# A list-scheduled attention and FFN kernel: low parts and sums of the FFN's second product shared out anew between VectorE and GpSimd, its first product's last two parts set later, and longer ways between engines in the planner

## The chip, the cores and the metric

One NeuronCore of one Trainium2 chip runs the whole program. The metric is the device time of one execution in microseconds, the median of three runs; the profile is of one further execution. TensorE is PE in the rows (its weight loads are PEld), VectorE is DVE, ScalarE is ACT, GpSimd is POOL, and SyncE, which issues most DMAs, is SP.

## The reference

Causal attention in blocks of 64 over 64 batch-and-head pairs, then a two-layer FFN with a leaky rectifier whose slope `alpha` is given for each hidden unit, all in float32:

```python
# q, k, v: (8, 8, 576, 64); w_in: (512, 2048); w_out: (2048, 512); alpha: (2048,)
scores = 1/sqrt(64) * q @ k.T;  mask: block(i) >= block(j), block of 64
attn = softmax(scores);         x = attn @ v, laid out as (4608 tokens, 512)
h = x @ w_in
g = np.maximum(h, 0.0) + alpha * np.minimum(h, 0.0)
out = g @ w_out
```

## The kernel before

Matrix products run on float32 values split in two: a high part that TensorE takes in its reduced float32 format (`fp32r`) and a low part, the rest. A product is then three: high by high, high by low, low by high. `split` makes the parts: ScalarE casts the high part (line 532), and VectorE or GpSimd subtracts it from the value to get the low part (line 533).

The program has two phases. In the first, attention (lines 979 to 1124) is mixed with the FFN of the first six of the sixteen blocks of 128 hidden units, in chunks of 256 tokens (lines 646 to 679). The other ten blocks, five pairs, come in the second phase in nine rounds of 512 tokens, and both of its products use the Winograd form of Strassen's scheme: seven products of quarter matrices in place of eight.

A round of the second phase has two halves that overlap with those of its neighbours:

- `pair1`, for each of the five pairs of blocks: seven products of six matmuls each (line 722), on three PSUM banks x, y and z. They are numbered 0 to 6 here, as in the code before: x takes 0, 2, 4 and 5, y takes 1, z takes 3 and 6. Between them other engines read the banks: `keep` (ScalarE, line 731) copies x after product 0 (u1), after 2 (u2) and after 4 (u3), and product 2, 4 or 5 may go on adding into x only when that copy is done. VectorE adds z to u3 (line 753), and product 6 may go on in z only after that. `onto` (VectorE, line 735) adds u1 into y and u2 into z. `act` applies the rectifier (ScalarE line 739, VectorE line 740) and leaves four quarters `c` of the hidden values in SBUF.
- `chunk2`, for the 512 tokens: seven products, each a chain of five blocks (one for each pair, index g) of six matmuls (line 780). A block needs the high part `gh` (ScalarE, line 532) and the low part `gl` (line 533) of a quarter or of a sum of quarters. The sums are in `plus` (line 765): three for each pair ahead of product 2 (`second`), one ahead of product 6 (`sums`). Both parts have six buffers. Before the change a low part is made by VectorE for g = 1 and 3 and by GpSimd for g = 0, 2 and 4; in the last round all but g = 0 are VectorE's.

For the next round, `factors` makes sums of quarters of the 512 tokens' input (VectorE, line 549) and splits seven of them: low parts named X, 128 by 512, of which VectorE makes three and GpSimd four (line 533 too).

The order of every engine's instructions is set ahead by `Plan.schedule`, a list scheduler. It keeps a ready queue for each engine by priority (a position on the PE's time axis, such as `turn + k` for product k of `pair1`, `turn + g` for a block of `chunk2` and `t - LEAD` for its split), reckons a cost for every operation (`c_dve`, `c_pool`, `c_act`, and so on), lets a result be seen by another engine `LAT` nanoseconds after its end, and issues what is ready. The engines then run these orders in order, waiting on semaphores. The table `SHIFTS` moves the priorities of single operations of the first phase; the second phase's priorities (from 2.0e6) have no entry in it.

Of the kernel before, what the change touches and what calls it, by code (L numbers as in the profile page):

```python
# [29 lines left out]
CHA = 256  # L30
# [8 lines left out]
BANKS, HB, AB, HT, AM, AT, WB = 7, 2, 2, 3, 2, 3, 4  # L39
LEAD, AHEAD2, XB2, W2N, CN = 6, 12, 10, 11, 6  # L40
# [72 lines left out]
LAT = {"PE": 250, "DVE": 130, "ACT": 140, "POOL": 140}  # L113
# [24 lines left out]
class Plan:  # L138


    def __init__(self):
        self.ops, self.writer, self.readers = [], {}, {}
        self.free, self.tiles, self.quota, self.last = {}, {}, {}, {}
# [11 lines left out]
    def op(self, engine, cost, fn, r=(), w=(), prio=0.0, claim=(), then=None, ends=()):  # L155
# [24 lines left out]
        self.ops.append((engine, cost, fn, deps, bufs, prio, then))  # L180
        return i

    def schedule(self):
# [43 lines left out]
        while events:  # L227
# [13 lines left out]
            for engine, heap in ready.items():  # L241
# [42 lines left out]
                lat = LAT.get(engine, 0)  # L284
# [35 lines left out]
def c_dve(n):  # L320
    return 65 + n / 0.96

# [54 lines left out]
def attn_ffn(ctx, tc, qT, kT, vT, w_in, w_out, alpha, out):  # L377
# [152 lines left out]
    def split(src, hi, lo, n, r, hk, lk, claim, on, prio):  # L530

        op("ACT", c_act(n, True), lambda: nc.scalar.copy(out=hi(), in_=src()), r=r, w=[hk], claim=claim, prio=prio)  # L532
        op(on, c_pool(n) if on == "POOL" else c_dve(n), lambda: (nc.gpsimd if on == "POOL" else nc.vector).tensor_tensor(  # L533
            out=lo(), in0=src(), in1=hi().bitcast(F32), op=ALU.subtract), r=[*r, hk], w=[lk], claim=claim, prio=prio)
# [12 lines left out]
    def add(e, n, to, a, b, f, prio, r=()):  # L547

        op(e, c_pool(n) if e == "POOL" else c_dve(n), lambda: (nc.gpsimd if e == "POOL" else nc.vector).tensor_tensor(  # L549
# [159 lines left out]
    def pair1(f, X, turn):  # L709
# [18 lines left out]
        def keep(bank):  # L728

            u = Buf("g")  # L730
            op("ACT", c_act(CHA), lambda: nc.scalar.copy(out=u(), in_=bank()[:, :CHA]), r=[bank], w=[u], prio=FP)
            return u
# [20 lines left out]
        op("DVE", c_dve(CHA), lambda: nc.vector.tensor_tensor(out=u3(), in0=z()[:, :CHA], in1=u3(), op=ALU.add), r=[z], w=[u3], prio=FP)  # L753
        act(f + 1, u3, u3, cs[3])
        product(x, "22", "t4", 5, False)
        act(f + 1, x, lambda: x()[:, :CHA], cs[2])
        product(z, "s4", "22", 6, False)
# [4 lines left out]
    def chunk2(t0, cs, turn, last):  # L762

        def plus(to, a, b, f, on, prio):
            op(on, c_pool(CHA) if on == "POOL" else c_dve(CHA), lambda: (nc.gpsimd if on == "POOL" else nc.vector).tensor_tensor(  # L765
                out=to(), in0=a(), in1=b(), op=f), r=[a, b], w=[to], prio=prio)

        def product(k, bank, c, at, first):

            for g in range(NG):  # L770
# [4 lines left out]
                split(v, gh, gl, CHA, [v], gh, gl, [], "DVE" if g % 2 or last and g else "POOL", t - LEAD)  # L775
# [37 lines left out]
        def second(g, prio):  # L813

            c11, c12, _, c22, s3 = cs[g]
            plus(s3, c11, c12, ALU.subtract, "DVE", prio)
            plus(c12, c12, c22, ALU.add, "DVE", prio)
            plus(c11, c12, c11, ALU.subtract, "DVE", prio)
# [452 lines left out]
```

## Time and profile before

| | us |
| --- | --- |
| median of three runs | 1119.76 (1118.62 to 1120.52) |
| the profiled execution | 1117.95 |
| span of its instructions | 1115.8 |
| PE busy, PEld busy | 1073.9, 969.9 |
| DVE busy | 814.1 |
| ACT busy | 701.4 |
| POOL busy | 666.2 |
| mean granted TensorE clock | 0.998 |

PE is busy for nearly the whole span, but the ends of its matmuls are modelled, so a stall shows as a gap only where it is longer than what the pipeline hides, and PEld, or the count of matmuls in a stretch, tells more. Attention ends and the second phase begins near 625 us; a round of it is about 53.5 us from then on, so one look at a round stands for the others. A number of nanoseconds after the bar in a group's row is the mean of one instruction; the numbers behind the second bar are the engine's idle time just before the group's instructions, and what ended it.

### The profile page before, as it was taken

Reading aid. Unit: us, or ns where it says so; the run is one execution under the profiler, and the core shown is the slowest. Engines: PE = TensorE matmul, PEld = TensorE weight load, DVE = VectorE, ACT = ScalarE, POOL = GpSimd, SP = SyncE. Lnnn points to the kernel's source line nnn. Section 1 sums busy time; section 2 is a strip of 40 time slices with the busy share of each in tenths; the row PEclk is TensorE's granted clock in tenths of the full one; section 3 lists DMA queues with packets and bytes.
Section 4 is the critical chain, followed back from the end, with each engine's and each line's share of the span. In section 5 each row is a group of like instructions: output and inputs, shape, how many; then the busy total and the mean of one; then the engine's idle time right before and its main releaser. Section 6 shows DMA issues by size and latency. Waiting matters only on the chain.

```text
span 1115.8 us, 24537 instructions
## 1 busy us (share of the span) xinstructions
PE 1073.9 (96%) x8158; PEld 969.9 (87%) x8158; DVE 814.1 (73%) x1779; ACT 701.4 (63%) x1969; POOL 666.2 (60%) x837
## 2 busy tenths in 40 slices
PE   7999999999999999999999989999999999999998
PEld 4668888888888888898888889999989898989998
DVE  8886685676575745757558598879696969787776
ACT  7788877776666766758555564555455555545554
POOL 4767757667676666666489574636272736364522
PEclk9999999999999999999999999999999999999999
DMA  6687886876668795749044436767676868686875
GB/s 193 194 257 214 233 246 169 267 209 194 193 176 248 217 270 157 214 140 271 32 175 152 174 119 199 243 212 243 211 253 202 276 193 280 188 267 196 270 259 162
DMA packets 139486, 233.37 MB, mean 209 GB/s; under 512 B 14816, under 2 KB 51680, under 8 KB 139360
## 3 DMA queue, kind: packets, MB, share of 16 engines
q1 hardware_dynamic: 138928, 231.53, 68.0%
q8 instruction: 65, 1.06, 0.4%
q14 instruction: 61, 0.50, 0.1%
q10 hardware_dynamic: 432, 0.27, 0.1%
HBM read 150.22 MB, written 37.49 MB: 168 GB/s over the span
## 4 chain that ended last, share of the span: by engine, by line
PE 85%; DVE 9%; ACT 2%; issue 2%; DMA 1%; POOL 1%; DVEq 0%; ACTq 0%; POOLq 0%
PE bank L780 17%; PE bank L722 16%; PE bank L646 13%; PE bank L679 13%; PE bank L1120 8%; PE bank L979 6%; PE bank L1019 6%; PE bank L1049 2%; DVE X L533 2%; DVE c L765 2%; PE bank L1076 1%; DVE xt L549 1%; DVE bank L735 1%; PE bank L984 1%; DVE gl L533 1%
## 5 line engine op out<-in xcount | busy, mean ns | idle before, releaser
L722 PE MATMUL bank<-X,w 128*128 128x256 f32 x1890 | 251.7, 284 | 23.0 <-DVE g L753 13.0
L722 PEld LDWEIGHTS bank<-X,w 128*128 128x128 f32 x1890 | 235.2, 189 | 28.8 <-DVE g L753 15.2
L780 PE MATMUL bank<-w,gh 128*128 128x256 f32 x1260 | 228.9, 280 | 0.8 <-ACT gh L532 0.8
L1011 POOL TENSOR_SCALAR p<-p,ri 128x256 f32<-128x256 f32 (+3 forms) x256 | 141.3, 567 | 90.9 <-DVE ri L1009 42.5
L780 PEld LDWEIGHTS bank<-w,gh 128*128 128x128 f32 x1260 | 193.6, 189 | 1.0 <-ACT gh L532 1.0
L780 PE MATMUL bank<-w,gl 128*128 128x256 f32 x630 | 177.6, 282 | 3.5 <-DVE gl L533 3.5
L533 POOL TENSOR_TENSOR gl<-c,gh 128x256 fp32r<-128x256 f32 x112 | 95.2, 855 | 121.4 <-ACT gh L532 120.3
L1003 ACT ACTIVATE p<-bank,nm 128x256 f32<-128x256 f32 (+3 forms) x256 | 133.9, 532 | 28.2 <-DVE nm L1000 13.8
L679 PE MATMUL bank<-wa,gh 128*128 128x512 f32 x432 | 140.1, 405 | 0.0
L646 PE MATMUL bank<-xh,wa 128*128 128x256 f32 x864 | 128.0, 287 | 0.0
L780 PEld LDWEIGHTS bank<-w,gl 128*128 128x128 f32 x630 | 118.9, 189 | 4.7 <-DVE gl L533 4.7
L532 ACT CAST gh<-c 128x256 fp32r<-128x256 f32 x198 | 79.7, 407 | 62.6 <-PE bank L780 60.6
L646 PEld LDWEIGHTS bank<-xh,wa 128*128 128x128 f32 x864 | 113.6, 190 | 2.7 <-issue 0.9
L1019 PE MATMUL bank<-ident,p 128*128 128x128 f32 x640 | 100.2, 277 | 5.0 <-POOL p L1011 2.9
L666 POOL TENSOR_TENSOR gl<-g,gh 128x256 fp32r<-128x256 f32 x108 | 83.2, 773 | 32.4 <-ACT gh L663 26.7
L1000 DVE TENSOR_REDUCE nm<-bank 128x1 f32<-128x384 f32 (+3 forms) x144 | 80.4, 587 | 22.5 <-PE bank L979 18.8
L979 PE MATMUL bank<-K,Q 128*128 128x512 f32 (+1 forms) x448 | 94.5, 331 | 1.1 <-ACT pl L1063 0.9
L1120 PE MATMUL bank<-PTF,vraw 128*64 128x320 f32 (+3 forms) x768 | 94.1, 384 | 0.5 <-ACT PTF L1096 0.5
L1019 PEld LDWEIGHTS bank<-ident,p 128*128 128x128 f32 x640 | 76.0, 142 | 16.8 <-POOL p L1011 6.6
L659 DVE SCALAR_TENSOR_TENSOR g<-g,oal,bank 128x256 f32<-128x256 f32 x108 | 51.4, 476 | 48.3 <-ACT g L657 47.9
L679 PEld LDWEIGHTS bank<-wa,gh 128*128 128x128 f32 x432 | 75.6, 189 | 12.4 <-issue 0.5
L679 PE MATMUL bank<-wa,gl 128*128 128x512 f32 x216 | 85.8, 397 | 0.1
(162 smaller groups left out, 2210.4 us busy)
## 6 DMA issues: line engine op xcount, KB each, us to landing
w<-wd SPq DMA_DIRECT2D x315, 256.0 KB, 4.0
Q<-QH SPq DMA_DIRECT2D x56, 256.0 KB, 3.9
K<-KH SPq DMA_DIRECT2D x112, 128.0 KB, 3.8
vraw<-in_v SPq DMA_DIRECT2D x32, 320.0 KB, 3.7
qraw<-in_q SPq DMA_DIRECT2D x30, 320.0 KB, 4.0
xd<-xT SPq DMA_DIRECT2D x8, 1152.0 KB, 6.5
part<-o SPq DMA_DIRECT2D x36, 256.0 KB, 3.5
xb<-xd SPq DMA_DIRECT2D x9, 1024.0 KB, 7.9
```

The costliest lines, as they stand in the source:

```text
L533: op(on, c_pool(n) if on == "POOL" else c_dve(n), lambda: (nc.gpsimd if on == "POOL" else nc.vector).tensor_tensor(out=lo(), in0=src(), in ...
L646: nc.tensor.matmul(hp()[:, :n], ww()[:, 0, cc * P:(cc + 1) * P], x()[:, cc, :n], start=(i == 0 and cc == 0), stop=(i == 2 and cc == NCC - 1))
L666: op("POOL", c_pool(CHA), lambda: nc.gpsimd.tensor_tensor(out=gl(), in0=g(), in1=gh().bitcast(F32), op=ALU.subtract), r=[g, gh], w=[gl], p ...
L679: nc.tensor.matmul(acc(), a()[:, ts], ww(), start=(first and i == 0), stop=(last and i == 2))
L722: nc.tensor.matmul(bank()[:, :CHA], W()[:, i, 256 * at + P * c:256 * at + P * c + P], B()[:, j, CHA * c:CHA * c + CHA], start=(first and n ...
L780: nc.tensor.matmul(bank()[:, CHA * i:CHA * i + CHA], a()[:, P * i:P * i + P], W()[:, x], start=(first and g + i + n == 0), stop=(g == NG - ...
L979: nc.tensor.matmul(o, Q()[:, i, qs], K()[:, 2 * h + i, :w], start=(i == 0), stop=(i == 1))
L1000: op("DVE", c_dve(w), lambda h=h: nc.vector.tensor_reduce(out=nm()[:, h:h + 1], in_=sb[h]()[:, off[h]:off[h] + w], axis=AX.X, op=ALU.max, ...
L1003: op("ACT", 238 + w / 1.2, lambda h=h, t=t: nc.scalar.activation(out=t()[:, :w], in_=sb[h]()[:, off[h]:off[h] + w], func=AF.Exp, bias=nm() ...
L1011: op("POOL", 244 + w / 1.2, lambda h=h: nc.gpsimd.tensor_scalar(out=pts[h]()[:, :w], in0=pts[h]()[:, :w], scalar1=ri()[:, h:h + 1], scalar ...
L1019: nc.tensor.transpose(out=tp()[:, base + c * P:base + (c + 1) * P], in_=pts[h]()[:, c * P:(c + 1) * P], identity=ident)
L1120: nc.tensor.matmul(ob()[rows[h], a - q0:q1 - q0], V()[:, c, h, :], moving, start=(c == 0), stop=(c == cs[-1][0]))
```

## The change

Four things change together.

- Low parts of `chunk2`: VectorE keeps only g = 1 (`LO_DVE`); g = 0, 2, 3 and 4 are GpSimd's. The last round is as before. In eight rounds that is 56 subtractions.
- Sums of `chunk2` (`SUMS`): two of the three sums of `second` go from VectorE to GpSimd, 90 in all, and the sum of product 6 goes from GpSimd to VectorE, 45 in all.
- In `pair1` products 5 and 6 get the priorities `turn + 6` and `turn + 7` in place of `turn + 5` and `turn + 6`.
- The planner's reckoning: `LAT` is longer for every engine, so that first-phase orders change too; a two-input SBUF operation on VectorE costs 65 + 1.3 n in place of 65 + n / 0.96; and the results of `keep`, of the sum of z and u3, and of the low parts of `chunk2` are reckoned with 500 ns more (`SLACK`) before another engine sees them. These numbers set the order alone.

The lines of the changed kernel stand 11 further down in this part of the code: 722 is 733, 753 is 764, 765 is 776, 780 is 791.

```diff
+SSN, SLACK = 1.3, 500
+SUMS, LO_DVE = ("DVE", "POOL", "POOL", "DVE"), (1,)
...
-LAT = {"PE": 250, "DVE": 130, "ACT": 140, "POOL": 140}
+LAT = {"PE": 320, "DVE": 200, "ACT": 220, "POOL": 220}
...
-        self.ops, self.writer, self.readers = [], {}, {}
+        self.ops, self.writer, self.readers, self.slack = [], {}, {}, []
...
-    def op(self, engine, cost, fn, r=(), w=(), prio=0.0, claim=(), then=None, ends=()):
+    def op(self, engine, cost, fn, r=(), w=(), prio=0.0, claim=(), then=None, ends=(), slack=0):
...
+        self.slack.append(slack)
...
-                lat = LAT.get(engine, 0)
+                lat = LAT.get(engine, 0) + self.slack[chosen]
...
+class SS(float):
+    pass
+
+
+def c_ss(n):
+    return SS(65 + n * SSN)
+
+
...
-    def split(src, hi, lo, n, r, hk, lk, claim, on, prio):
+    def split(src, hi, lo, n, r, hk, lk, claim, on, prio, slack=0):
...
-        op(on, c_pool(n) if on == "POOL" else c_dve(n), lambda: (nc.gpsimd if on == "POOL" else nc.vector).tensor_tensor(
-            out=lo(), in0=src(), in1=hi().bitcast(F32), op=ALU.subtract), r=[*r, hk], w=[lk], claim=claim, prio=prio)
+        op(on, c_pool(n) if on == "POOL" else c_ss(n), lambda: (nc.gpsimd if on == "POOL" else nc.vector).tensor_tensor(
+            out=lo(), in0=src(), in1=hi().bitcast(F32), op=ALU.subtract), r=[*r, hk], w=[lk], claim=claim, prio=prio, slack=slack)
...
-        op(e, c_pool(n) if e == "POOL" else c_dve(n), lambda: (nc.gpsimd if e == "POOL" else nc.vector).tensor_tensor(
+        op(e, c_pool(n) if e == "POOL" else c_ss(n), lambda: (nc.gpsimd if e == "POOL" else nc.vector).tensor_tensor(
...
         def keep(bank):
...
-            op("ACT", c_act(CHA), lambda: nc.scalar.copy(out=u(), in_=bank()[:, :CHA]), r=[bank], w=[u], prio=FP)
+            op("ACT", c_act(CHA), lambda: nc.scalar.copy(out=u(), in_=bank()[:, :CHA]), r=[bank], w=[u], prio=FP, slack=SLACK)
...
         product(z, "s1", "t1", 3, True)
         product(x, "s3", "t3", 4, False)
         u3 = keep(x)
-        op("DVE", c_dve(CHA), lambda: nc.vector.tensor_tensor(out=u3(), in0=z()[:, :CHA], in1=u3(), op=ALU.add), r=[z], w=[u3], prio=FP)
+        op("DVE", c_dve(CHA), lambda: nc.vector.tensor_tensor(out=u3(), in0=z()[:, :CHA], in1=u3(), op=ALU.add), r=[z], w=[u3], prio=FP, slack=SLACK)
         act(f + 1, u3, u3, cs[3])
-        product(x, "22", "t4", 5, False)
+        product(x, "22", "t4", 6, False)
         act(f + 1, x, lambda: x()[:, :CHA], cs[2])
-        product(z, "s4", "22", 6, False)
+        product(z, "s4", "22", 7, False)
...
         act(f, z, lambda: z()[:, :CHA], cs[1])
...
         def plus(to, a, b, f, on, prio):
-            op(on, c_pool(CHA) if on == "POOL" else c_dve(CHA), lambda: (nc.gpsimd if on == "POOL" else nc.vector).tensor_tensor(
+            op(on, c_pool(CHA) if on == "POOL" else c_ss(CHA), lambda: (nc.gpsimd if on == "POOL" else nc.vector).tensor_tensor(
...
-                split(v, gh, gl, CHA, [v], gh, gl, [], "DVE" if g % 2 or last and g else "POOL", t - LEAD)
+                split(v, gh, gl, CHA, [v], gh, gl, [], "DVE" if g in LO_DVE or last and g else "POOL", t - LEAD, SLACK)
...
         def second(g, prio):
...
-            plus(s3, c11, c12, ALU.subtract, "DVE", prio)
-            plus(c12, c12, c22, ALU.add, "DVE", prio)
-            plus(c11, c12, c11, ALU.subtract, "DVE", prio)
+            plus(s3, c11, c12, ALU.subtract, SUMS[0], prio)
+            plus(c12, c12, c22, ALU.add, SUMS[1], prio)
+            plus(c11, c12, c11, ALU.subtract, SUMS[2], prio)
...
         product(5, x, lambda g, prio: cs[g][3], 4, False)
...
-        product(6, z, sums(2, 2, 0, ALU.subtract, "POOL"), 3, False)
+        product(6, z, sums(2, 2, 0, ALU.subtract, SUMS[3]), 3, False)
```

What the scheduler makes of it, at three places of a round in the middle of the second phase. First PE, at the last pair of a round (weights `w13_7265`). In both orders the rows of line 722 or 733 are products 4, 5 and 6, told apart by the bank: x for 4 and 5, z for 6. Four rows of line 780 or 791 are one block of `chunk2`. Before, from product 4 to product 6:

```order
L722 MATMUL bank2_184<-X3_6770,w13_7265 128x256 x6
L780 MATMUL bank0_178<-w211_7288,gh2_680 128x256 x2
L780 MATMUL bank0_178<-w211_7288,gl2_698 128x256
L780 MATMUL bank0_178<-w211_7288,gh2_680 128x256 x2
L780 MATMUL bank0_178<-w211_7288,gl2_698 128x256
L780 MATMUL bank0_178<-w212_7290,gh3_824 128x256 x2
L780 MATMUL bank0_178<-w212_7290,gl3_840 128x256
L780 MATMUL bank0_178<-w212_7290,gh3_824 128x256 x2
L780 MATMUL bank0_178<-w212_7290,gl3_840 128x256
L722 MATMUL bank2_184<-X6_7252,w13_7265 128x256 x6
L722 MATMUL bank7_145<-X5_7247,w13_7265 128x256 x6
```

After, from the second block behind product 4 (which and whose first block stand just ahead of these rows) to product 6:

```order
L791 MATMUL bank1_180<-w29_7267,gh0_537 128x256 x2
L791 MATMUL bank1_180<-w29_7267,gl0_552 128x256
L791 MATMUL bank1_180<-w29_7267,gh0_537 128x256 x2
L791 MATMUL bank1_180<-w29_7267,gl0_552 128x256
L733 MATMUL bank3_186<-X6_7255,w13_7265 128x256 x6
L791 MATMUL bank4_205<-w210_7275,gh1_566 128x256 x2
L791 MATMUL bank4_205<-w210_7275,gl1_574 128x256
L791 MATMUL bank4_205<-w210_7275,gh1_566 128x256 x2
L791 MATMUL bank4_205<-w210_7275,gl1_574 128x256
L733 MATMUL bank2_184<-X0_6729,w13_7265 128x256 x6
```

Between products 4 and 6 stood two blocks and product 5; now there are three blocks and product 5. Ahead of this piece, between products 1 and 4 of the same pair, stood products 2 and 3 and one block, and now there are products 3 and 2 and three blocks.

Second VectorE, at the same pair: from the addition of u1 into y to the sum of z and u3, on which product 6 waits. `X` are low parts of factors, `xt` a sum of factors. Before:

```order
L735 TENSOR_TENSOR bank7_145<-bank7_145,g6_6804 128x256
L765 TENSOR_TENSOR c11_7482<-c5_7359,c11_7482 128x256
L533 TENSOR_TENSOR X2_6753<-xt1_6726,X2_6753 128x512
L740 SCALAR_TENSOR_TENSOR o1_1191<-g4_6761,oal_83,bank7_145 128x256
L549 TENSOR_TENSOR xt1_6726<-xb0_6610,xt1_6726 128x512
L533 TENSOR_TENSOR X4_7241<-xt0_6712,X4_7241 128x512
L753 TENSOR_TENSOR g1_598<-bank1_180,g1_598 128x256
```

After:

```order
L746 TENSOR_TENSOR bank5_211<-bank5_211,g2_715 128x256
L751 SCALAR_TENSOR_TENSOR c10_7439<-g6_6799,oal_83,bank7_145 128x256
L544 TENSOR_TENSOR X2_6777<-xt1_6758,X2_6777 128x512
L751 SCALAR_TENSOR_TENSOR o1_1248<-g0_506,oal_83,bank5_211 128x256
L560 TENSOR_TENSOR xt1_6758<-xb0_6618,xt1_6758 128x512
L544 TENSOR_TENSOR X3_6790<-xt0_6723,X3_6790 128x512
L544 TENSOR_TENSOR gl2_732<-c12_7487,gh2_727 128x256
L776 TENSOR_TENSOR raw0_158<-c16_7576,c10_7439 128x256
L764 TENSOR_TENSOR g4_6756<-bank2_184,g4_6756 128x256
```

One sum of quarters (765) has left its place behind the addition, and a low part, another sum and one more step of the rectifier now stand in the piece.

Third VectorE, a little later, ahead of the addition of u1 into y for the first pair of the next round; the rows of lines 793 and 798 (804 and 809) add a finished product to the output. Before:

```order
L798 TENSOR_TENSOR m1_290<-bank5_211,m1_290 128x512
L765 TENSOR_TENSOR c16_7582<-c17_7546,c16_7582 128x256
L533 TENSOR_TENSOR gl1_631<-raw0_158,gh1_610 128x256
L765 TENSOR_TENSOR raw0_158<-o1_1191,raw0_158 128x256
L765 TENSOR_TENSOR raw0_158<-raw0_158,o0_1179 128x256
L533 TENSOR_TENSOR gl3_840<-c4_7326,gh3_824 128x256
L765 TENSOR_TENSOR o1_1191<-raw0_158,o1_1191 128x256
L793 TENSOR_TENSOR m2_6785<-bank4_207,m2_6785 128x512
L735 TENSOR_TENSOR bank0_178<-bank0_178,g6_6804 128x256
```

After:

```order
L746 TENSOR_TENSOR bank2_184<-bank2_184,g5_6771 128x256
L751 SCALAR_TENSOR_TENSOR raw0_158<-g2_715,oal_83,bank2_184 128x256
L544 TENSOR_TENSOR gl1_574<-raw0_158,gh1_566 128x256
L776 TENSOR_TENSOR raw0_158<-o1_1248,raw0_158 128x256
L804 TENSOR_TENSOR m2_6817<-bank4_205,m2_6817 128x512
L776 TENSOR_TENSOR o1_1248<-o1_1248,c11_7511 128x256
L746 TENSOR_TENSOR bank6_225<-bank6_225,g6_6799 128x256
```

Four sums and two low parts ahead of the addition have become two sums and one low part. On GpSimd, last, the work behind the four X of a round. Before, from the first X on (the sums in it are those of product 6):

```order
L533 TENSOR_TENSOR X1_6733<-xb0_6610,X1_6733 128x512
L533 TENSOR_TENSOR X3_6770<-xb0_6610,X3_6770 128x512
L533 TENSOR_TENSOR X5_7247<-xb0_6610,X5_7247 128x512
L533 TENSOR_TENSOR gl3_840<-c2_7331,gh3_824 128x256
L533 TENSOR_TENSOR X6_7252<-xt1_6726,X6_7252 128x512
L533 TENSOR_TENSOR gl5_1138<-o1_1191,gh5_1120 128x256
L533 TENSOR_TENSOR gl0_506<-c15_7503,gh0_495 128x256
L765 TENSOR_TENSOR raw0_158<-raw0_158,c12_7462 128x256
L533 TENSOR_TENSOR gl2_698<-raw1_176,gh2_680 128x256
L533 TENSOR_TENSOR gl4_951<-c7_7379,gh4_944 128x256
L533 TENSOR_TENSOR gl5_1138<-c11_7482,gh5_1120 128x256
L765 TENSOR_TENSOR c15_7503<-c15_7503,c11_7482 128x256
```

After, the last twelve of the 22 rows that begin with the first X (four X, twelve low parts and six sums):

```order
L544 TENSOR_TENSOR gl2_732<-c13_7479,gh2_727 128x256
L544 TENSOR_TENSOR gl3_852<-raw0_158,gh3_841 128x256
L776 TENSOR_TENSOR c0_7227<-c5_7350,c0_7227 128x256
L776 TENSOR_TENSOR c6_7418<-c1_7320,c6_7418 128x256
L776 TENSOR_TENSOR c9_7430<-c9_7430,o0_1227 128x256
L776 TENSOR_TENSOR c8_7398<-c8_7398,o0_1227 128x256
L544 TENSOR_TENSOR gl5_1120<-c6_7418,gh5_1098 128x256
L776 TENSOR_TENSOR c4_7332<-c9_7430,c4_7332 128x256
L776 TENSOR_TENSOR c3_7298<-c8_7398,c3_7298 128x256
L544 TENSOR_TENSOR gl0_552<-c4_7332,gh0_537 128x256
L544 TENSOR_TENSOR gl1_574<-c3_7298,gh1_566 128x256
L544 TENSOR_TENSOR gl2_732<-raw1_176,gh2_727 128x256
```

In the rows before, sums stand singly between low parts; now six of them, the new ones of `second`, stand close together, each with the low part that needs it some rows behind.

## The prediction

> **What bounds the kernel now.** I read the page first (busy times and the chain that ended last), then the engines by stretches, then who PE waited for, and last the chain through one round.
>
> ```profile
> PE 1073.9 (96%) x8158; PEld 969.9 (87%) x8158; DVE 814.1 (73%) x1779; ACT 701.4 (63%) x1969; POOL 666.2 (60%) x837
> PE 85%; DVE 9%; ACT 2%; issue 2%; DMA 1%; POOL 1%; DVEq 0%; ACTq 0%; POOLq 0%
> ```
>
> PE carries the chain; the change leaves its matmuls as they are, so only stalls can be won. The 9% of DVE in the chain is where PE stood still for it. Two rounds of the second phase (the first and the last of six alike), its first stretches, and one near its end, in the columns stretch, length, PE, PEld, DVE, ACT, POOL, clock, DMA:
>
> ```profile
> 600.00:650.00 50.00, 46.97 (x312) 42.07 (x311) 35.76 (x66) 26.95 (x68) 37.24 (x40) 1.00 0.48 155
> 650.00:700.00 50.00, 44.91 (x365) 43.65 (x364) 43.37 (x78) 27.08 (x74) 27.12 (x27) 1.00 0.54 167
> 703.40:757.00 53.60, 50.93 (x422) 50.28 (x422) 43.75 (x78) 28.93 (x77) 27.17 (x31) 1.00 0.72 227
> 971.20:1024.70 53.50, 50.84 (x422) 50.18 (x422) 43.72 (x78) 28.93 (x77) 27.11 (x31) 1.00 0.73 232
> 1050.00:1100.00 50.00, 50.00 (x421) 49.96 (x420) 37.86 (x77) 26.53 (x71) 16.94 (x21) 1.00 0.82 269
> ```
>
> The stretch at 1050 has 421 matmuls in 50 us with PE full: 118.8 ns each. A round has 420 (35 products and 35 blocks of six), so 49.9 us of work in 53.55 us: 3.65 us are lost in each. From 650 to 700 it is 365 x 118.8 ns = 43.4 us of work, 6.6 us lost. Who PE waited for in six rounds (us, times, longest):
>
> ```profile
> PE bank L722 <- DVE g L753: 7.7, 6, 1.3
> PE bank L722 <- ACT g L731: 5.0, 6, 0.9
> PE bank L780 <- DVE gl L533: 3.5, 6, 0.6
> ACT g L739 <- DVE bank L735: 29.9, 24, 2.6
> ```
>
> Each of the three happens once a round: 1.28, 0.83 and 0.58 us, 2.7 us together. The other 0.95 us of the 3.65 is the pipeline's own start after a stall, some 0.3 us for each, which is shorter than the gaps that are listed. Where the first two come from shows in the chain through 20 us of one round (start, length, what):
>
> ```profile
> 864.42 1.43 PE bank L722 x12
> ...
> 865.94 0.43 DVE bank L735
> 866.37 1.39 DVE c L765
> 867.76 0.60 DVE X L533
> 868.36 0.07 DVE c L740
> ...
> 868.68 1.40 DVE xt L549
> 870.08 1.69 DVE X L533
> 871.76 0.35 DVE g L753
> ...
> 872.15 0.98 PE bank L722 x6
> ...
> 879.85 0.95 DVE c L765
> 880.81 0.60 DVE m L793
> 881.41 0.35 DVE bank L735
> ...
> 882.06 0.38 ACT g L731
> ...
> 882.48 0.97 PE bank L722 x6
> ```
>
> At the last pair of a round products 0 and 1 end at 865.85; from then DVE works without a pause, from the addition into y to the sum for product 6, and product 6 can start only at 872.15. At the next pair the addition into y stands behind DVE's sums; ACT, which has a step of the rectifier ahead of its copy of x, waits for that addition, and PE for the copy. So PE is held by DVE's queue, not by a distance: other pairs have the same distances and no stall.
>
> **The change, part by part: DVE and POOL.** In rounds of the middle VectorE gives up 7 low parts and 10 sums and gets 5 sums. What they cost, from the groups of the six rounds (the number behind the comma is the mean in ns) and from each line by itself (min, median and max in ns):
>
> ```profile
> L533 POOL TENSOR_TENSOR gl<-c,gh 128x256 fp32r<-128x256 f32 x78 | 66.1, 854 | 76.3 <-ACT gh L532 75.4
> L765 POOL TENSOR_TENSOR c<-c,c 128x256 f32<-128x256 f32 x15 | 11.8, 792 | 3.4 <-DVE gl L533 3.4
> L765 DVE TENSOR_TENSOR c<-c,c 128x256 f32<-128x256 f32 x25 | 18.4, 735 | 0.2
> L533 DVE TENSOR_TENSOR gl<-c,gh 128x256 fp32r<-128x256 f32 x50 | 30.8, 615 | 10.1 <-ACT gh L532 9.7
> L740 DVE SCALAR_TENSOR_TENSOR c<-g,oal,bank 128x256 f32<-128x256 f32 x61 | 28.9, 474 | 9.8 <-ACT g L739 9.8
> L532 ACT CAST gh<-c 128x256 fp32r<-128x256 f32 x128 | 51.6, 407 | 40.6 <-PE bank L780 39.6 <-POOL gl L533 0.6
> ...
> L765 DVE TENSOR_TENSOR c<-c,c x25: 406/834/1493, 711.9 to 1018.6; 128x256 f32<-128x256 f32 x25
> L533 POOL TENSOR_TENSOR gl<-c,gh x78: 732/852/1197, 714.3 to 1024.6; 128x256 fp32r<-128x256 f32 x78
> L533 POOL TENSOR_TENSOR X<-xb,X x18: 1292/1459/1754, 705.4 to 976.8; 128x512 fp32r<-128x512 f32 x18
> L533 DVE TENSOR_TENSOR X<-xt,X x12: 679/1221/1773, 706.9 to 977.0; 128x512 fp32r<-128x512 f32 x12
> ```
>
> DVE loses 7 x 0.615 + 5 x 0.735 = 8.0 us of 43.7 a round; POOL gains 7 x 0.854 + 5 x 0.79 = 9.9 us on 27.1, so 37 us in a round that may not be shorter than 49.9. Neither engine is full.
>
> But the same DVE sum takes 0.41 us at the least and 1.49 at the most, and POOL's low part 0.73 to 1.20: operations whose inputs lie in SBUF wait for the other engine's. POOL is busy 27.1 of 53.55 us now (51%) and would be so 37 of some 51 (73%). DVE's sum now costs 0.33 us over its least at 51%; in proportion it would cost 0.47 at 73%, hence 0.88 us, and a low part 0.70. Then 29 operations that take 14 x 0.615 + 15 x 0.735 = 19.6 us become 17 that take 7 x 0.70 + 10 x 0.88 = 13.7 us: 5.9 us less in place of 8.0. I take this value, since both ends of the proportion are rows of this stage; bounds are no dearer at all (8.0) and the longest rows throughout (in rival (a)).
>
> The Trainium skill, "SBUF — State Buffer", section "SBUF: two separate sides", says it harder: VectorE with two SBUF inputs and GpSimd share a port pair by an exclusive lock, and the loser blocks for the whole instruction. The rows with 0.41 beside 1.49 us agree. By that rule alone the time when either holds the pair is what counts: with the least durations, POOL's 21 low parts, 5 sums and 4 X with DVE's 29 and 3 X hold it 24.2 + 13.8 = 38.0 us of 53.55 before, and after, with POOL's 28 low parts, 10 sums and 4 X and DVE's 17 and 3 X, 33.0 + 8.9 = 41.9 us of 49.9 (an estimate). That is an argument against the change, but it still leaves room for a round without stalls.
>
> **PE's order at the three stalls.** The last pair: from the end of product 1 to product 6 there stood products 2, 3, 4 and 5 and three blocks, seven pieces of six matmuls or 0.713 us each: 5.0 us, and with the stall the 6.30 us of the chain (865.85 to 872.15). After, it is the same four products and six blocks, ten pieces or 7.1 us. DVE's work in that time loses a sum (1.39) and gains a step of the rectifier, a low part and a sum, 0.47 + 0.62 + 0.74 = 1.83 us: 6.30 + 0.44 = 6.7 us against 7.1. Hidden, with 0.4 us to spare, if the two X and the `xt` don't get slower; with the longest row for the X that took 0.60 (1.77) it stalls for 0.8 us. I keep 0.5 us of stall and start here on average.
>
> The next pair's copy of x: ahead of the addition into y stand two sums less and one low part less, about 2 us by the means; the stall was 0.83. Gone. The low part that PE waited for 0.58 us was one of VectorE's in the same queue: gone likewise, and what VectorE still makes (g = 1) has a later user. Products 5 and 6, set one later, and the 500 ns put on the two results that PE waited for are what brings blocks in between; they add no instruction.
>
> Covers: VectorE's backlog was POOL's idle time (76.3 us of waiting before low parts in six rounds). What is late next is POOL. Its heaviest stretch is the 22 rows behind the first X: 4 x 1.46 + 12 x 0.854 + 6 x 0.79 = 20.8 us. Their users on PE, with 118.8 ns a matmul, stand 15 us apart in the order, so the stretch must start with 5.8 us in hand. The six buffers let the low part just ahead of it be made some 8.8 us before its use; less the cast (0.41 us by ACT) and itself (0.85) that is 7.5 us. 1.7 us to spare over 22 operations: 0.08 us on each eats it.
>
> I leave 0.8 us of stall a round (0.5 above, 0.3 for POOL and what I can't see): 3.65 - 0.8 = 2.85 us won, in the seven rounds with the stalls (six, and the two stalls that follow at 1024.7): 20.0 us. The first round, 650 to 700, loses 6.6 us, partly because the weights are still being split; of that I take 3. The stretch from 600, where products have no blocks to stand between, I leave.
>
> **The first phase** is ordered anew by the longer `LAT`. PE's waits there, the first two and the last of 14 groups up to 640 us, 12.7 us in all:
>
> ```profile
> PE bank L1019 <- POOL p L1011: 2.9, 2, 2.6
> PE bank L984 <- DVE xT L903: 2.3, 1, 2.3
> ...
> PE bank L984 <- ACT PTF L1096: 0.2, 1, 0.2
> ```
>
> There is hardly anything to win, and much of it is the start, where no order helps. What could be lost is bounded by a first phase as leaky as the second: 3.65 us in 53.55 over 600 us, 41 us. In the order the least PE work between a hidden product (line 646) and the second product that waits for its low part grows from 2.7 to 4.0 us, and that between a score and the transposes that wait for GpSimd's scaling from 3.4 to 4.1 (estimates, matmuls counted and weighed by their spacing here). So I stay near the row: 0, with -3 to +5.
>
> Sum: 1117.95 (span 1115.8 and 2.15 around it) - 20.0 - 3 = 1095. The median of the runs is 1.8 above that execution: 1096.8, so 1097.
>
> **Rivals.** (a) The port eats it. POOL at 73% makes DVE's X and `xt` take their longest: at the last pair 6.7 + 1.2 (the short X) + 0.2 (low part, sum) = 8.1 us against 7.1, a stall of 1.0, nearly as before, and one of the others stays in part. Against it: 5.9 us less work on DVE. Won is about 1.3 us a round, 9 us: 1110. The lock of the skill's SBUF page is this rival's mechanism.
>
> (b) GpSimd becomes the bound, and the kernel slower. The place is the same 22 rows, the blocks of `chunk2` behind the new sums. They have 1.7 us to spare; to cost more than the 3.65 us that can be won they must take 5.4 us more, 0.25 each, a low part 1.10 us on the mean in place of 0.854. The longest is 1.20, so it could be, but the median is 0.852 and DVE's operations in SBUF get fewer. At 1.20 throughout, 0.35 x 22 - 1.7 = 6.0 us are lost a round against 3.65 won: 16 us over seven rounds, 1136; a time just past the point, 1125, is likelier.
>
> (c) The first phase leaks. `SHIFTS` holds values for single operations, and orders made with other latencies may suit them less. A third of the bound, 14 us, would leave 1111; the static distances speak against it.
>
> (d) The change doesn't do what it says: product 6 still waits for VectorE just as long. Seven rounds as before, 1117 to 1120. The added blocks between 4 and 6 speak against it.
>
> **How the numbers follow.** Forecast (most stalls of the rounds go): 0.70, with a range of its own of 1089 to 1104. (a) 0.13, (c) 0.05, (d) 0.04, (b) 0.08. The low end is all of the 25.6 us in seven rounds and 5 of the first round's, 1089; the high end takes in (a) and (c), 1111. What a measurement of this kernel can tell from no change is about 0.2%, 2.2 us. Faster: 0.70 + 0.13 + 0.04 of (c) = 0.87; the same 0.05; slower 0.08.
>
> **What would show it.** Rounds of about 50.7 us; the row of line 764 (753 before) as releaser of PE gone or under 0.5 us a round; the releaser 731 (742) gone; DVE near 38 and POOL near 37 us a round; sums on DVE near 0.88 us. Wrong would be: rounds above 52 us, PE waiting for POOL's low parts (line 544), or PE's waits before 600 us well over 13 us.

## The result and the profile after

The changed kernel takes 1095.14 us (median of four runs, 1093.28 to 1095.81) against 1119.76: a ratio of 0.9778, with a 95% interval from 0.9761 to 0.9795. The profiled execution took 1094.58 us, its instructions 1092.8. The forecast was 1097, in a range from 1089 to 1111. Of all executions timed for this document one, of the kernel with the longer `LAT` alone, took 1783.52 us at a mean granted clock of 0.63; its ratio in the table below leaves that one out.

From the page, busy times and the shares of the chain that ended last:

```profile
PE 1066.0 (98%) x8158; PEld 964.9 (88%) x8158; DVE 769.5 (70%) x1678; ACT 701.0 (64%) x1969; POOL 746.1 (68%) x938
PE 83%; DVE 9%; ACT 2%; issue 2%; DMA 2%; POOL 1%; ACTq 0%; DVEq 0%; POOLq 0%
```

PE's matmuls are the same 8158, and 101 instructions more than before are GpSimd's (146 given by VectorE, 45 taken back). One round and the sum over six, in the columns of the prediction's windows:

```profile
760.20:810.80 50.60, 49.89 (x422) 49.69 (x421) 38.40 (x67) 29.00 (x78) 36.42 (x42) 1.00 0.77 245
sum 304.50, PE 300.39 PEld 299.01 DVE 229.41 ACT 174.61 POOL 218.97; mean PE 50.07 PEld 49.84 DVE 38.24 ACT 29.10 POOL 36.49
```

304.50 us for six rounds are 50.75 each; before it was 53.55. Who PE waited for in these six rounds:

```profile
PE bank L733 <- DVE g L764: 4.1, 6, 0.7
```

No other wait of PE's is listed there. Of three stalls a round two are gone (line 742, the copy of x, and line 544, VectorE's low part); product 6 of the last pair still waits 0.7 us for VectorE's addition of z to u3, in place of 1.28.

Where the 23.0 us between the two spans come from is told by counting matmuls in fixed stretches. Before, then after:

```profile
600.00:700.00 100.00, 91.87 (x674) 85.73 (x673) 79.12 (x143) 54.03 (x141) 64.36 (x67) 1.00 0.51 161
700.00:1050.00 350.00, 331.67 (x2742) 327.32 (x2742) 288.27 (x512) 190.19 (x506) 182.35 (x201) 1.00 0.73 231
```

```profile
600.00:700.00 100.00, 95.11 (x709) 89.42 (x708) 77.34 (x134) 56.97 (x148) 81.41 (x88) 1.00 0.54 176
700.00:1050.00 350.00, 345.36 (x2904) 343.77 (x2903) 262.09 (x455) 201.21 (x531) 251.10 (x290) 1.00 0.78 249
```

With 118.2 ns a matmul (350 us hold 2960 of them when PE never waits, as a run below shows), 162 more matmuls from 700 to 1050 are 19.2 us, and 35 more from 600 to 700 are 4.1. That makes 23.3; the first 600 us (4230 matmuls, 4235 before) and the tail gave nothing, -0.3.

### The profile page after: what moved, and what is told of

Its sections match the earlier page's. It is cut to its first block, busy times and chain, and to the rows that moved or that the text cites. A ratio compares the mean times of both kernels' runs of the same rounds, so it can differ in the third digit from the quotient of the medians.

```text
span 1092.8 us, 24551 instructions
## 1 busy us (share of the span) xinstructions
PE 1066.0 (98%) x8158; PEld 964.9 (88%) x8158; DVE 769.5 (70%) x1678; ACT 701.0 (64%) x1969; POOL 746.1 (68%) x938
## 4 chain that ended last, share of the span: by engine, by line
PE 83%; DVE 9%; ACT 2%; issue 2%; DMA 2%; POOL 1%; ACTq 0%; DVEq 0%; POOLq 0%
PE bank L791 17%; PE bank L733 16%; PE bank L657 13%; PE bank L690 13%; PE bank L1131 8%; PE bank L1030 6%; PE bank L990 6%; PE bank L1060 2%; DVE X L544 2%; PE bank L1087 1%; DMA raw<-in_w_in 1%; ACT X L543 1%; DVE gl L544 1%; DVE xh L643 1%; DVE xt L560 1%
## 5 line engine op out<-in xcount | busy, mean ns | idle before, releaser
L1014 ACT ACTIVATE p<-bank,nm 128x384 f32<-128x384 f32 (+3 forms) x256 | 134.0, 532 | 34.5 <-DVE nm L1011 18.0
L544 POOL TENSOR_TENSOR gl<-c,gh 128x256 fp32r<-128x256 f32 x135 | 116.8, 876 | 37.3 <-ACT gh L543 34.8
L543 ACT CAST gh<-c 128x256 fp32r<-128x256 f32 x196 | 77.1, 408 | 39.6 <-PE bank L791 29.6
L1011 DVE TENSOR_REDUCE nm<-bank 128x1 f32<-128x512 f32 (+3 forms) x144 | 80.8, 585 | 25.0 <-PE bank L990 20.7
L750 ACT ACTIVATE g<-bank 128x256 f32<-128x256 f32 x135 | 51.9, 385 | 58.9 <-DVE bank L746 55.3
```

The lines of the kernel that those rows point to most:

```text
L544: op(on, c_pool(n) if on == "POOL" else c_ss(n), lambda: (nc.gpsimd if on == "POOL" else nc.vector).tensor_tensor(out=lo(), in0=src(), in1 ...
L1014: op("ACT", 238 + w / 1.2, lambda h=h, t=t: nc.scalar.activation(out=t()[:, :w], in_=sb[h]()[:, off[h]:off[h] + w], func=AF.Exp, bias=nm() ...
```

## The experiments

All ratios are to the kernel before. In the table, "lost" is 350 us less 118.2 ns for each matmul between 700 and 1050 us: seven rounds. The last column is the count of matmuls from 600 to 700 us, where the second phase starts.

| kernel | us | ratio (95%) | lost in 700–1050 | 600–700 |
| --- | --- | --- | --- | --- |
| before | 1118.6 to 1119.8 | 1 | 25.8 | 674 |
| the change | 1095.14 | 0.9778 (0.9761–0.9795) | 6.6 | 709 |
| without the sharing | 1103.38 | 0.9863 (0.9847–0.9879) | 14.7 | 701 |
| the sharing alone | 1110.64 | 0.9929 (0.9916–0.9942) | 17.9 | 673 |
| with the old `LAT` | 1105.9 | 0.9878 (0.986–0.9896) | 10.9 | 660 |
| with the old costs, no slack | 1107.12 | 0.9895 (0.9878–0.9912) | 14.7 | 667 |
| old priorities of products 5, 6 | 1094.6 | 0.9787 (0.9774–0.9801) | 6.6 | 709 |
| the longer `LAT` alone | 1120.58 | 1.0013 (1.0004–1.0022) | 25.5 | 667 |
| SBUF operations at 65 + 1.9 n | 1097.8 | 0.9816 (0.9803–0.983) | 8.9 | 708 |
| one X from VectorE to GpSimd | 1102.23 | 0.9851 (0.9836–0.9866) | 9.2 | 673 |
| all low parts on GpSimd | 1098.31 | 0.9816 (0.98–0.9833) | 9.1 | 700 |
| `SLACK` 900 | 1090.26 | 0.9749 (0.9729–0.9769) | 0 | 673 |
| 65 + 1.5 n and `SLACK` 700 | 1098.02 | 0.9815 (0.9799–0.9831) | 11.1 | 712 |
| `SLACK` 900, first round shared anew | 1094.15 | 0.9783 (0.977–0.9796) | 0 | 657 |

**The order without the sharing.** The edit:

```diff
-SUMS, LO_DVE = ("DVE", "POOL", "POOL", "DVE"), (1,)
+SUMS, LO_DVE = ("DVE", "DVE", "DVE", "POOL"), (1, 3)
```

> The changed kernel with the sharing undone: low parts of g = 1 and 3 and the three sums of product 2 on VectorE, product 6's sum on GpSimd, as before; longer latencies, slack and later priorities stay. PE's order keeps its blocks between products 4, 5 and 6. Theory A (the distances in PE's order remove the stalls): two of the three stalls of a round stay away, the last pair's is 0.7 to 1.5 us, rounds 50.7 to 51.5 us, 1095 to 1102. Theory B (VectorE's relief removes them): VectorE is busy some 44 us a round again, rounds over 52.5 us, 1108 or more.

**The sharing without the order**: `LAT`, the costs, the slack and the two priorities as before.

```diff
-SSN, SLACK = 1.3, 500
+SSN, SLACK = 1 / 0.96, 0
...
-LAT = {"PE": 320, "DVE": 200, "ACT": 220, "POOL": 220}
+LAT = {"PE": 250, "DVE": 130, "ACT": 140, "POOL": 140}
...
-        product(x, "22", "t4", 6, False)
+        product(x, "22", "t4", 5, False)
...
-        product(z, "s4", "22", 7, False)
+        product(z, "s4", "22", 6, False)
```

> The kernel before with the new sharing alone: VectorE gives 7 low parts and net 5 sums a round to GpSimd; PE's order in a round is as before (one block between 4 and 5, none between 5 and 6). Theory A: the last pair's stall stays near 1 us and some of the others stay, rounds 52 to 53.5 us, 1109 to 1119. Theory B: VectorE near 38 us a round, the stalls behind its sums gone, rounds under 51.5 us, 1095 to 1103.

Neither does it alone. PE's waits from 709 to 1024 us, six rounds, first of the order alone, then of the sharing alone:

```profile
PE bank L733 <- DVE g L764: 6.5, 7, 1.0
PE bank L733 <- ACT g L742: 3.9, 6, 0.7
```

```profile
PE bank L733 <- DVE g L764: 8.7, 12, 0.8
PE bank L733 <- ACT g L742: 1.2, 1, 1.2
```

The order alone keeps the addition and the copy as releasers, with shorter waits, and lies between the two theories: 14.7 us lost in 350 make rounds of some 51.8 us. The sharing alone removes the low part, and the copy but for one wait, and has the addition (764) hold PE twice a round; its 1110.64 us lie in theory A's range. Of the 25.8 us in seven rounds the order wins 11.1 and the sharing 7.9, together 19.0. The two together won 19.2, so in the rounds they add up.

**The old `LAT`** in the changed kernel, and **the old costs without slack**:

```diff
-LAT = {"PE": 320, "DVE": 200, "ACT": 220, "POOL": 220}
+LAT = {"PE": 250, "DVE": 130, "ACT": 140, "POOL": 140}
```

> The changed kernel with the old LAT. The first phase is ordered nearly as before; PE's order in a steady round is like the changed kernel's. Theory A and B both: steady rounds 50.5 to 51 us. If the longer latencies gain nothing elsewhere: 1094 to 1097; if the 4 us won from 0 to 100 and 600 to 700 us come from them: 1098 to 1100.

```diff
-SSN, SLACK = 1.3, 500
+SSN, SLACK = 1 / 0.96, 0
```

> The changed kernel with SLACK = 0 and the old cost of VectorE's SBUF operations (65 + n / 0.96). PE's order becomes 4, two blocks, 5, 6 and one block behind, so products 5 and 6 stand together; the sharing is the new one. Theory A: the last pair's stall is back at 1.0 to 1.5 us and the sum for product 6 stalls at other pairs too, rounds 51.2 to 52.5 us, 1099 to 1109. Theory B: as the changed kernel, 1093 to 1097.

Each costs some 11 to 13 us, by the medians or by the ratios. Without the longer `LAT` neither its rounds (some 51.3 us) nor its time came as expected: 4.3 us are lost again in the seven rounds, where the waits listed grow from 4.1 us to 5.5, and 49 matmuls, 5.8 us, between 600 and 700. PE's longest waits from 600 to 709 us, with the old `LAT` and then in the changed kernel:

```profile
PE bank L733 <- ACT g L742: 3.2, 3, 1.6
PE bank L791 <- POOL gl L544: 1.7, 2, 1.4
PE bank L733 <- DVE g L764: 1.0, 1, 1.0
```

```profile
PE bank L733 <- ACT g L742: 3.0, 5, 0.8
PE bank L733 <- DVE g L764: 1.8, 2, 1.3
```

The copy of x holds PE about as long in both; what the old `LAT` adds are GpSimd's low parts (1.7 us for 0.2) and some short waits, and a fall of the clock:

```profile
650.00:700.00 50.00, 43.33 (x337) 41.61 (x336) 40.14 (x65) 25.23 (x69) 36.34 (x39) 0.97 0.54 168
```

The mean clock of 0.97 in this stretch takes 1.5 of the 5.8 us (more on it at the longer `LAT` alone). In the rounds the addition holds PE no longer at the last pair but at another, where VectorE had itself just waited 1.46 us for a sum of GpSimd's (824.6 to 826.1 us in one round). What the longer `LAT` does between 600 and 700 us is not shown further.

With the old costs and no slack 8.1 us are lost again in the seven rounds, and 5.0 between 600 and 700. PE's waits from 709 to 1024 us:

```profile
PE bank L733 <- ACT g L742: 5.2, 6, 1.1
PE bank L733 <- DVE g L764: 3.4, 8, 0.5
```

The time lies in theory A's range, but not by its mechanism: the addition holds PE for 0.5 us at most, and it is the copy of x that is back.

**The old priorities.**

```diff
-        product(x, "22", "t4", 6, False)
+        product(x, "22", "t4", 5, False)
...
-        product(z, "s4", "22", 7, False)
+        product(z, "s4", "22", 6, False)
```

> The changed kernel with products 5 and 6 back at `turn + 5` and `turn + 6`. PE's order in the steady rounds is the same as with the later priorities. If the order is what counts (the blocks between 4 and 6 come from the planner's costs and slack alone), it measures like the changed kernel, 1093 to 1097 us, and a steady round stays at 50.75 us. If the later priorities do something that the pattern of products and blocks doesn't show, a part of the 2.9 us won in each round is lost again: over 1099.

They do nothing: 2904 matmuls from 700 to 1050 us and 709 from 600 to 700, as with them.

**The longer `LAT` alone**, in the kernel before:

> The kernel before with the longer `LAT` alone. Taking the longer `LAT` out of the changed kernel cost 11 us, some 6 of them in 650 to 700 us. Theory A, `LAT` acts by itself on the start of the second phase and on the rounds: 1108 to 1112, with the stretch 650 to 700 losing 4 to 5 us in place of 7 and rounds at 52.8 to 53.2 us (its order has two blocks between 3 and 4 like that of the costs and slack). Theory B, `LAT` works only together with the sharing, because VectorE's queue holds PE whatever the order is: rounds stay at 53.5 and the whole lies at 1115 to 1119.

It wins nothing, as theory B said, and lies even a little above its range. But the rounds did not stay as they were: PE's waits over six rounds show another pattern, and PE around the stall at 766 us another clock (stretches of 2 us, columns as before, the clock third from the end):

```profile
PE bank L722 <- DVE g L753: 14.3, 6, 2.4
```

```profile
764.00:766.00 2.00, 2.00 (x19) 1.99 (x17) 2.00 (x3) 1.20 (x3) 1.43 (x2) 1.00 0.74 248
766.00:768.00 2.00, 0.20 (x2) 0.00 (x0) 2.00 (x4) 0.00 (x0) 0.38 (x1) 1.00 0.83 262
768.00:770.00 2.00, 1.42 (x11) 1.42 (x11) 2.00 (x7) 1.44 (x4) 0.65 (x1) 0.92 0.38 129
770.00:772.00 2.00, 2.00 (x11) 2.00 (x11) 2.00 (x5) 0.97 (x4) 2.00 (x3) 0.50 0.25 30
772.00:774.00 2.00, 2.00 (x15) 2.00 (x15) 1.69 (x5) 0.71 (x3) 1.09 (x2) 0.72 0.70 149
774.00:776.00 2.00, 2.00 (x20) 2.00 (x19) 1.67 (x2) 1.11 (x3) 1.94 (x4) 1.00 0.95 302
```

The three stalls of a round have become one, 2.39 us at the last pair, and behind it the granted clock falls to half for some 3.4 us. It does so in four of the seven rounds. 3.4 us at half clock cost 1.7. The changed kernel loses 0.94 us a round where the wait listed is 0.68, so a wait costs some 0.26 us more than its length (called start here). 7 x (2.39 + 0.26) + 4 x 1.7 = 25.4, the 25.5 of the table.

**Dearer operations in SBUF** and **one X on GpSimd**, both aimed at the stall that the change leaves:

```diff
-SSN, SLACK = 1.3, 500
+SSN, SLACK = 1.9, 500
```

> The changed kernel with a two-input SBUF operation on VectorE reckoned at 65 + 1.9 n, 551 ns at 256 and 1038 at 512, in place of 398 and 731 (measured in the changed kernel: 0.73 to 0.75 us and 1.15 us in the mean). If the stall that is left, product 6 of the last pair behind VectorE's two X, comes from the planner's reckoning these too short, it goes or halves: 0.5 to 0.95 us in each of seven rounds, 1088 to 1092. If the irregular order that comes of it (no block between 5 and 6 in two of five pairs) opens new stalls, 1095 to 1103.

```diff
-        for x, on in zip(XS, ("DVE", "POOL", "DVE", "POOL", "DVE", "POOL", "POOL")):
+        for x, on in zip(XS, ("DVE", "POOL", "DVE", "POOL", "POOL", "POOL", "POOL")):
```

> The changed kernel with the X of t1, the 128x512 low part that stands just ahead of the sum of z and u3 at a round's last pair, made by GpSimd (1.4 us) in place of VectorE (1.2 us). If VectorE's work there is what holds product 6, 1.2 us less of it removes the stall of 0.7 us: 1088 to 1092. If the shared port pair gives GpSimd's X back to VectorE as longer operations, or GpSimd's 22 rows get their 1.4 us out of the 1.7 us to spare and PE waits for its low parts, 1095 to 1103, with POOL's gl as releaser.

In both the stall at the last pair is gone and a new one has come, of 0.9 and 1.1 us, at another product (the X on GpSimd, six rounds):

```profile
PE bank L733 <- ACT g L742: 6.4, 6, 1.1
```

In the rounds it isn't GpSimd's low parts that hold PE, as one theory had it, but the copy of x again. The kernel with the X on GpSimd loses more, 4.3 us, from 600 to 700 (673 matmuls for 709), where its longest wait, 2.0 us, is for a low part of GpSimd's and the clock falls to half for 3.4 us, 1.7 of the 4.3. Both edits changed PE's order as well, so they do not show by themselves that VectorE's work is the cause.

**All low parts on GpSimd**, with PE's pattern of products and blocks kept:

```diff
-SUMS, LO_DVE = ("DVE", "POOL", "POOL", "DVE"), (1,)
+SUMS, LO_DVE = ("DVE", "POOL", "POOL", "DVE"), ()
```

> The changed kernel with VectorE's last low parts of `chunk2` (g = 1) given to GpSimd too; PE's pattern of products and blocks in the steady rounds stays as in the changed kernel. Theory, VectorE's work ahead of the sum of z and u3 holds product 6 at a round's last pair: one low part (0.9 us there) less in front of it takes the stall of 0.7 us and its restart away, 1087 to 1090 us. Rival, GpSimd is near its own bound: with 5 low parts more it is busy 41 us a round, its 22 rows have no time to spare, and PE waits for its low parts: 1095 to 1105.

Both theories are right in part. VectorE's addition no longer holds PE, though products and blocks stand there as in the changed kernel: so it was VectorE's work that held product 6. From the addition into y to that of z and u3 it takes 6.2 us (804.11 to 810.26) in place of 7.6, the low part's 0.96 less and 0.55 off the sum. But GpSimd holds PE now, and a cast just ahead of it, some 14 us behind the last pair (six rounds; GpSimd is 284.78 us busy of 350 from 700 to 1050):

```profile
PE bank L791 <- POOL gl L544: 3.2, 6, 0.5
PE bank L791 <- ACT gh L543: 1.8, 6, 0.3
```

**More slack**, alone and with dearer operations:

```diff
-SSN, SLACK = 1.3, 500
+SSN, SLACK = 1.3, 900
```

> The changed kernel with `SLACK` 900 in place of 500: eight blocks in place of six between products 1 and 6 of a round's last pair (one more between 4 and 5, one more between 5 and 6), three for two between 4 and 5 elsewhere, and none between 5 and 6 of three pairs. If distance is all that the last stall lacks, 1087 to 1091. If the blocks put there are missing elsewhere (six blocks for each pair are all there are), a stall opens at another product, as with the dearer SBUF operations: 1094 to 1102.

```diff
-SSN, SLACK = 1.3, 500
+SSN, SLACK = 1.5, 700
```

> The changed kernel with both a little further: a two-input SBUF operation on VectorE at 65 + 1.5 n, `SLACK` 700. Seven blocks between products 1 and 6 of the last pair in place of six. If the planner's numbers only need to come nearer to the durations measured, all stalls of the steady rounds go: 1087 to 1091. If the total of VectorE's and GpSimd's work around the change of rounds sets the loss and the order only moves it, 1093 to 1100.

With `SLACK` 900 PE waits for nothing in the rounds:

```profile
700.00:1050.00 350.00, 350.00 (x2960) 350.00 (x2959) 257.44 (x459) 200.32 (x542) 256.87 (x297) 1.00 0.78 254
```

The share of the work is that of the change, so distance in the order is enough to win all that was left, 6.6 us. By the spans 3.2 us arrive (1089.6 for 1092.8): from 600 to 700 us there are 673 matmuls in place of 709, 4.3 us back, 1.7 of them by a fall of the clock behind a wait of 1.7 us. With 65 + 1.5 n and 700 in its place the rounds lose 11.1 us, most of it again at the copy of x:

```profile
PE bank L733 <- ACT g L742: 6.2, 6, 1.2
```

Numbers nearer to the durations are not what counts; the order that comes out of them is.

**The first round**: `SLACK` 900, and VectorE makes g = 1 and 3 in the first round of `chunk2` alone.

```diff
-                split(v, gh, gl, CHA, [v], gh, gl, [], "DVE" if g in LO_DVE or last and g else "POOL", t - LEAD, SLACK)
+                split(v, gh, gl, CHA, [v], gh, gl, [], "DVE" if g in (LO_DVE if t0 else (1, 3)) or last and g else "POOL", t - LEAD, SLACK)
```

> The kernel with `SLACK` 900, and in the first round of `chunk2` alone the low parts of g = 3 made by VectorE again. Its steady rounds stay as they are, without a stall. What it still loses after the first phase is 643 to 676 us, where PE waits twice for 1.6 to 1.7 us for a low part of GpSimd's, which splits the last weights there too; the clock drops to half for some 3 us behind the second. If GpSimd's load is the cause, both shrink and the clock stays at 1: 3 to 5 us less, 1085 to 1087. If VectorE's queue holds GpSimd's sums there anyway (its sums wait for steps of the rectifier), 1089 to 1092.

Neither theory: the rounds stay at 0, the start gets worse, 657 matmuls. PE's waits from 600 to 709 us:

```profile
PE bank L733 <- DVE g L764: 3.1, 3, 2.0
PE bank L791 <- POOL gl L544: 2.0, 2, 1.6
```

Of the two waits for a low part the second is down to 0.4 us, the first stays at 1.6, and a wait of 2.0 us for VectorE has come between them, with the clock at half behind it. So VectorE's time is as short there as GpSimd's. `SLACK` 900 as it was is the best of these kernels; its ratio's interval and that of the change still overlap a little, and the two were not timed in one group, so that it beats the change is likely and not shown.

## Why the prediction was right, step by step

**PE bounds, only stalls can be won: right.** 19.2 of the 23.0 us lie in the seven rounds (20.0 forecast), 4.1 between 600 and 700 (3 forecast, for 650 to 700), and the rest gave -0.3 (0 forecast). From 650 to 700 alone it is 20 matmuls (385 for 365), 2.4 us. That the sum for the profiled execution, 1095, met 1094.58 is partly luck: too much in the rounds and too little at the start cancel. One reading was wrong. The 9% of VectorE in the chain, some 100 us, is not PE standing still: the waits listed for VectorE in the whole kernel before come to 21.4 us, and the share is still 9% after. The share says what the chain runs through; the waits say what can be won.

**Rounds of 50.7 us: right (50.75), by other parts than I gave.** I left 0.5 us of stall and start at the last pair and 0.3 for GpSimd. The last pair alone keeps 0.7 us of wait and some 0.26 of start, and GpSimd costs nothing. The step that was mis-sized is VectorE's work at the last pair, 6.7 us in my sum. VectorE there, one round (start, length, what; idle time is shown in brackets):

```profile
802.74 0.43 DVE L746 TENSOR_TENSOR bank<-bank,g 128x256 f32<-128x256 f32 x1 [0.84 <-PE bank L733]
803.22 0.48 DVE L751 SCALAR_TENSOR_TENSOR raw<-g,oal,bank 128x256 f32<-128x256 f32 x1
803.73 1.09 DVE L544 TENSOR_TENSOR X<-xt,X 128x512 fp32r<-128x512 f32 x1
804.75 0.47 DVE L751 SCALAR_TENSOR_TENSOR c<-g,oal,bank 128x256 f32<-128x256 f32 x1
805.14 1.40 DVE L560 TENSOR_TENSOR xt<-xb,xt 128x512 f32<-128x512 f32 x1
806.46 1.22 DVE L544 TENSOR_TENSOR X<-xt,X 128x512 fp32r<-128x512 f32 x1
807.60 0.96 DVE L544 TENSOR_TENSOR gl<-c,gh 128x256 fp32r<-128x256 f32 x1
808.49 1.51 DVE L776 TENSOR_TENSOR o<-raw,raw 128x256 f32<-128x256 f32 x1
809.92 0.41 DVE L764 TENSOR_TENSOR g<-bank,g 128x256 f32<-128x256 f32 x1
```

From the addition into y to that of z and u3 it is 7.6 us without a pause, and from the end of product 1 to the start of product 6 some 7.7, which stands against my 6.7. The two X are as long together as before (2.31 against 2.29 us); the low part took 0.96 where I put 0.62, and the sum 1.51 where I put 0.74: 1.1 us. GpSimd in that time:

```profile
807.09 1.19 POOL L544 TENSOR_TENSOR gl<-raw,gh 128x256 fp32r<-128x256 f32 x1
808.24 1.48 POOL L544 TENSOR_TENSOR X<-xb,X 128x512 fp32r<-128x512 f32 x1
```

VectorE's sum starts 0.25 us behind GpSimd's X and ends 0.28 behind its end. The shortest such sums take 0.41 us. That is rival (a)'s mechanism at one place: it gave a stall of 1.0 us there, and 0.7 stayed (I had named under 0.5 as the sign that I was right). But it had put 1.2 us on the X and 0.2 on low part and sum, and it was the other way round; and no other stall of VectorE's stayed in part, as it had expected. That the neighbour is the cause shows in all sums: of the 30 in these six rounds that took over 0.6 us and stand alone in the timeline, 29 end some 0.28 us behind the end of a GpSimd instruction, as do 47 of 48 before the change; of the sums under 0.6 us, 5 of 27 do and none of 42 before. With all low parts on GpSimd the sum at this place met a shorter instruction of GpSimd's and took 0.96 us in place of 1.51, again ending 0.29 us behind it.

**"A DVE sum 0.88 us": wrong on the mean.** All sums of line 776 in six rounds, on VectorE and on GpSimd, and one group's shortest, median and longest:

```profile
709.20:1013.70 304.50, 43.90 (x60) 45.53 (x60) 1.00 0.76 245
...
L776 DVE TENSOR_TENSOR c<-c,c x22: 409/421/961, 716.0 to 998.4; 128x256 f32<-128x256 f32 x22
```

0.73 us each, little more than the 0.71 of all 90 before (64.06 us), though GpSimd is busy 72% of a round and not 51%. My proportion of contention to GpSimd's busy share fails: half of this group ran within 12 ns of the least duration. What counts is which operation of the other engine an instruction meets. The Trainium skill, "SBUF — State Buffer", section "SBUF: two separate sides", says that the port pair shared by VectorE and GpSimd is locked for a whole instruction; lengths that cluster at 0.41, 0.69, 0.96 and 1.51 us, and the ends above, agree with that better than my proportion. VectorE's 38.2 us a round came out as forecast (38), by luck in part: seven low parts were dearer than my 0.70 (0.76 us each), ten sums cheaper than my 0.88, together 1.0 us less than I reckoned; against that, the records of neighbouring VectorE instructions overlap, by 3.6 us a round before and 2.8 after, so that busy time falls by less than the sum of what was taken away.

**"Products 5 and 6, set one later, and the 500 ns are what brings blocks in between": half wrong.** The priorities do nothing. The slack with the dearer costs does, and so does the longer `LAT`, to which I gave 0 because I looked for it in the first phase alone. In the first 600 us it does little and not one way: 9 matmuls more in the changed kernel (4230 for 4221), 17 fewer in the kernel before (4218 for 4235). From 600 to 1050 us, together with the rest, it is worth 10 of the 11 us between the spans (1103.8 without it). That term the forecast had put at nothing.

**Rivals.** (b) was not reached: PE waited for no low part in the rounds. The run with all low parts on GpSimd shows its edge: at 41 us a round (284.78 in seven) GpSimd holds PE for 0.5 us once in each, and with the cast 9.1 us are lost, still far from the 25.8 before. (c) did not come: before 600 us and after 1050 the two spans differ by 0.3 us, and PE's waits listed up to 640 us are 14.5 us in place of 12.7, not well over 13. (d) fell: the addition held PE for 4.1 us in six rounds in place of 7.7.

## What to carry to other kernels

Where PE waits in a list-scheduled kernel, the stall lies where one engine's queue and PE's order meet, so relieving the queue and widening the distance each only move or shorten it; the longer `LAT`, which won nothing alone, was worth 11 us among the other parts. Count the matmuls in a fixed stretch to see what was won, and list the releasers to see where the rest went, since a stall cured at one product comes back at the next if its blocks were taken from there. Estimate an operation that shares its way to SBUF by the neighbour that it meets, not by a mean.

## What was not expected of the hardware

PE's clock can halve after waits well below 3 us. In the run with the longer `LAT` alone, seven waits of 2.39 us, one a round, were followed in four rounds by some 3.4 us at half clock, a price of 1.7 us each. The three drops not shown yet:

```profile
870.00:880.00 10.00, 7.62 (x52) 7.42 (x51) 9.41 (x19) 4.30 (x12) 5.24 (x6) 0.83 0.50 158
930.00:940.00 10.00, 10.00 (x74) 10.00 (x73) 7.73 (x15) 4.74 (x13) 9.02 (x11) 0.83 0.57 171
1030.00:1040.00 10.00, 7.62 (x52) 7.41 (x51) 9.47 (x18) 4.34 (x12) 5.63 (x6) 0.83 0.50 154
```

No wait of up to 1.3 us in the rounds did this in any run, and one of 3.3 us at 650 us in the kernel with the sharing alone did not either.

What decides shows in when the drops begin: at 633.2, 769.7, 875.5, 930.1 and 1035.9 us in this run, which are 40, 31, 16 and 31 times 3.413 us apart. On a grid of such stretches the wait of 2.39 us lies nearly whole in one stretch ahead of each of the four drops in the rounds, and is split between two in the other three rounds. Four other kernels have a drop behind 670 us, each with a grid of its own. PE's idle time in the fullest stretches, from 620 to 1050 us:

| kernel | PE idle in a stretch, us | clock in the next |
| --- | --- | --- |
| the longer `LAT` alone | 2.31, 2.38, 2.27, 2.38 | 0.5 |
| one X on GpSimd | 2.23 | 0.5 |
| the old `LAT` | 1.98 | 0.5 |
| `SLACK` 900 | 1.97 | 0.5 |
| `SLACK` 900, first round shared anew | 1.85 | 0.5 |
| the old `LAT` | 1.72 | 1 |
| `SLACK` 900, first round shared anew | 1.61 | 1 |
| the longer `LAT` alone, other rounds | 1.58, 1.58, 1.53 | 1 |

The drop at 633.2 follows a stretch with 1.59 us and does not fit. For the rest it is not the length of a wait that decides, but how much of one stretch is idle: every stretch from 1.85 us on has a drop behind it, none up to 1.72 us has. The wait of 3.3 us, split in the middle, would leave 1.6 us in each; where the grid lay in that run is not known, and no run was made to test the rule.

The Trainium skill, "TensorE: Matmul & The Clock Gate", section "🔬 Part 1: The HAM clock gate (the "warmup" mystery)", has the clock set by activity in a free-running window of about 3.4 us; the drops' length, their distances and a drop in some rounds only agree with that. The rule of its section "HAM oscillation — how this bites in real kernels", to keep gaps below some 3.4 us, was not enough here.
